# Reordering the block products of the expert loop in a fused scan and routed-expert kernel

## The chip, the cores and the metric

The kernel runs on one core of a Trainium2 chip. A core has a matrix engine (TensorE, PE in the profile, with its weight loads as PEld), a vector engine (VectorE, DVE), a scalar engine (ScalarE, ACT), GpSimd (POOL) and SyncE (SP), which only issues transfers. Each engine executes its own list of instructions in order, and the lists meet at semaphores. The metric is the device time of one execution in microseconds, as the median of several runs; less is better.

## The reference, cut to what matters

The reference is a chunked state-space scan whose output, 3072 rows of 256 numbers, goes into a router with eight experts. Each row goes to the expert whose embedding has the largest cosine with it, through two matrices with a ReLU between them, and is scaled by its gate.

```python
xn = x / (np.linalg.norm(x, axis=-1, keepdims=True) + 1e-06)
logits = xn @ en.T / tau
expert_idx = np.argmax(logits, axis=1)
...
gate_w = probs[np.arange(N), expert_idx]
for e in range(E):
    mask = expert_idx == e
    ...
    h = np.maximum(x[mask] @ w1[e], 0.0)
    out[mask] = gate_w[mask, None] * (h @ w2[e])
```

Here N is 3072, E is 8, `w1[e]` is 256 by 1024 and `w2[e]` is 1024 by 256, all in fp32.

## The kernel before

The scan takes about the first 68 us and the sorting of rows by expert a few more; the change touches nothing there. Then come nine jobs. Job 0 and job 1 are parts of the first expert's rows and use ordinary products. Jobs 2 to 8 are the other seven experts in falling order of size; their row capacities are 416, 408, 400, 384, 368, 356 and 352. The function `expert(k, n, ...)` writes out the work of job n, and I call this "expert n". The order in which its lines stand is the order on every engine: the code records instructions one after the other, and nothing reorders them.

Each of the two matrix products of an expert is done in the Winograd form of Strassen's method: both operands are cut in 2 by 2 blocks, and seven block products stand for eight. This needs sums of blocks beforehand and additions afterwards:

- The first product (x times `w1`). `first_sum(i)`, i from 0 to 3, makes the sums of weight blocks on VectorE (tile `ws1`; number 2 overwrites a block of the weights). `first_tokens(i)` makes the sums of the turned rows `xT` (tile `t1`, in the trace `ts<-xT`). `first_product(p, i)`, i from 1 to 7, is block product i for pair p of the hidden features; a pair is two blocks of 128 hidden features, so a call is four instructions on TensorE in the trace. Products 1, 6, 7 and 4 of a pair go one after the other into the same PSUM region `a`, each on top of the last; 2 goes into `b`; 5 and 3 go into `e`. After each of 1, 6, 7 ScalarE copies `a` out (`first_keep`, line 974); after 4 it writes the ReLU of `a` (line 976). After 2, 5 and 3 VectorE adds such a copy to `b` or `e` (line 980), and ScalarE makes the ReLU in place (`first_relu`, line 986). The next product into a region can't begin before the copy out of it is done.
- The second product (hidden features times `w2`). `weight_sum(i)` and `token_sum(i, g)` make the sums on VectorE, `product(i)` the block products (eight instructions each), and `keep(i)` takes them out: 1, 6, 7 and 4 by ScalarE (lines 1034 and 1036), 2, 5 and 3 by VectorE (line 1040). Its products go in the order 1, 2, 6, 5, 7, 4, 3, so `keep(3)` is the last VectorE operation of an expert.

Around these stand: `past.out(parts)`, which turns the previous expert's result back by transposes on TensorE (line 1050), scales each part of 128 rows by its gate on ScalarE or, for odd parts, on VectorE, and scatters it by an indirect transfer issued by GpSimd (line 1056); part 0 needs only `keep(2)` and `keep(4)`, part 1 also needs `keep(3)`, since 128 to 255 reaches into the second half of the rows. `squares` and `gate_steps` make the gates: ScalarE squares, GpSimd takes a power (line 848), five small VectorE steps, an exponential on ScalarE (line 866), three more VectorE steps. `begin(n + 1)` gathers rows by GpSimd, `ahead.turn_x` turns the gathered rows of the next expert, `left_blocks` is a generator whose small VectorE steps are spread over the experts, and `rest(n)` has SyncE load weights two experts on. In expert 8 a GpSimd `drain` waits until the scatters issued so far have landed.

PSUM has eight banks. Five of them serve both matrix products through a ring, `k.bank["five"]`; three others, `turned`, serve the transposes.

Of the kernel before, what the change touches and what calls it, by code (L numbers as in the profile page):

```python
# [7 lines left out]
F32 = mybir.dt.float32  # L8
# [15 lines left out]
DM, E, F = NH * D, 8, 1024  # L24
# [801 lines left out]
class Job:  # L826
# [102 lines left out]
    def first_sum(s, i):  # L929
        k = s.k  # L930
        if i == 0:
            s.s1 = k.p.tile([128, 3, F // 2], F32, name="ws1", tag="ws1", bufs=1)
        w = lambda m, j: s.w1[:, j, F // 2 * m : F // 2 * m + F // 2]
        s.sums_of(i, [s.s1[:, q] for q in range(3)], w)

# [6 lines left out]
    def first_product(s, p, i):  # L942
        k, h = s.k, s.w // 2
        if p == 0 and i == 1:
            s.hT = k.p.tile([128, KF, CAP], F32, name="hT", tag="hT")
            s.pairs = [Net(), Net()]
        u = s.pairs[p]
        if i in (1, 2, 5):
            t = k.bank["five"]()
            setattr(u, {1: "a", 2: "b", 5: "e"}[i], t[:].rearrange("p (g c) -> p g c", g=2)[:, :, 0:h])  # L950
        w = lambda j, m: s.w1[:, j, F // 2 * m : F // 2 * m + F // 2]
        x = lambda j, n: s.xT[:, j, h * n : h * n + h]
        lhsT, rhs, out = {
            1: (w(0, 0), x(0, 0), "a"), 2: (w(1, 0), x(1, 0), "b"), 3: (s.s1[:, 2], x(1, 1), "e"),
            4: (w(1, 1), s.t1[:, 3], "a"), 5: (s.s1[:, 0], s.t1[:, 0], "e"), 6: (w(0, 1), s.t1[:, 1], "a"),
            7: (s.s1[:, 1], s.t1[:, 2], "a"),
        }[i]
        out = getattr(u, out)
        for g in range(2):
            f = 128 * (2 * p + g)  # L960
            k.nc.tensor.matmul(  # L961
                out[:, g], lhsT=lhsT[:, f : f + 128], rhs=rhs, start=(g == 0 and i in (1, 2, 5)), stop=True,
                skip_group_check=True,
            )
# [40 lines left out]
    def product(s, i, fs=range(KF // 2)):  # L1005
        k, h, half = s.k, s.w // 2, KF // 2
        if i == 1 and 0 in fs:
            s.y2 = [k.bank["five"](), k.bank["five"]()]
        a = s.y2[0][:, 0:h]
        b, e = s.y2[1][:, 0:h], s.y2[1][:, 256 : 256 + h]  # L1010
        out = (a, b, e, a, e, a, a)[i - 1]
# [27 lines left out]
            out, in0, q = {2: (c[0][0], b, 0), 5: (c[1][1], e, 2), 3: (c[0][1], e, 1)}[i]  # L1039
            nc.vector.tensor_tensor(out=out, in0=in0, in1=s.p[:, q], op=ALU.add)  # L1040

    def out(s, which=None):
        k, nc = s.k, s.k.nc
        for i, p in enumerate(s.parts):
            if which is not None and i not in which:
# [3 lines left out]
            for j in range(KD):  # L1049
                nc.tensor.transpose(t[:p, 128 * j : 128 * j + 128], s.yT[:, j, o : o + p], k.ident[:])  # L1050
            y = k.p.tile([128, DM], F32, name="yo", tag="yo", bufs=4)
            if i % 2:
                nc.vector.tensor_scalar_mul(y[:p], t[:p, 0:DM], s.gate[:p, i : i + 1])
            else:
                nc.scalar.activation(y[:p], t[:p, 0:DM], ACT.Copy, scale=s.gate[:p, i : i + 1])  # L1055
# [8 lines left out]
def ring(banks):  # L1064
    state = [0]

    def take():
        state[0] += 1
        return banks[(state[0] - 1) % len(banks)]

    return take
# [6 lines left out]
def moe(k):  # L1078
# [4 lines left out]
    turned = ring([banks[3], banks[6], banks[7]])  # L1083
    k.bank = {
        "hp": ring([banks[2], banks[0], banks[1]]), "xt": turned, "yp": ring(banks[4:6]), "ot": turned,
        "five": ring([banks[0], banks[1], banks[2], banks[4], banks[5]]),
    }
    last = NC - 1
    j0 = jobs[0]
    j0.turn_x(ring(banks[3:5]))  # L1090
# [46 lines left out]
    j = jobs[1]  # L1137
# [21 lines left out]
def expert(k, n, left, begin, rest):  # L1159
    nc, jobs = k.nc, k.jobs  # L1160
    j, past = jobs[n], jobs[n - 1]
    ahead = jobs.get(n + 1)
    j.first_product(0, 1)
    j.first_keep(0, 1)
    j.first_product(0, 2)
    j.first_keep(0, 2)
    j.first_product(0, 6)
    j.first_keep(0, 6)
    j.first_relu(0, 2)
    j.weight_sum(0)  # L1170
    j.first_product(0, 5)
    j.first_product(0, 7)
    j.first_keep(0, 7)
    j.first_keep(0, 5)
    j.first_product(1, 1)
    j.first_keep(1, 1)
    j.first_relu(0, 5)
    j.first_product(0, 4)
    j.first_keep(0, 4)
    j.first_product(1, 2)  # L1180
    j.first_keep(1, 2)
    j.first_product(0, 3)
    j.first_keep(0, 3)
    j.first_product(1, 6)
    j.first_keep(1, 6)
    j.first_relu(0, 3)
    j.first_relu(1, 2)
    j.weight_sum(1)
    j.token_sum(0, 0)
    j.first_product(1, 5)  # L1190
    j.first_product(1, 7)
    j.first_keep(1, 7)
    j.first_keep(1, 5)
    past.out((0, 1))
    j.first_relu(1, 5)
    past.out(range(2, past.nt))
    if n == E:
        nc.gpsimd.drain()
    j.first_product(1, 3)
    j.first_keep(1, 3)  # L1200
    j.first_relu(1, 3)
    j.first_product(1, 4)
    j.first_keep(1, 4)
    j.token_sum(1, 0)
    j.weight_sum(2)
    j.token_sum(0, 1)
    j.token_sum(1, 1)
    if n == E:
        k.blocks = nc.values_load(k.left[0][0:1, 1, 0:1], min_val=0, max_val=LEFT)
    j.product(1)  # L1210
    j.keep(1)
    j.product(2)
    j.keep(2)
    j.squares()
    j.token_sum(2, 0)
    j.token_sum(2, 1)
    if n + 1 < E:
        begin(n + 1)
    j.product(6)
    j.keep(6)  # L1220
    j.weight_sum(3)
    j.product(5)
    j.token_sum(3, 0)
    j.token_sum(3, 1)
    gates = j.gate_steps()
    next(gates)
    j.product(7)
    j.keep(7)
    j.keep(5)
    if ahead:  # L1230
        ahead.turn_x(act=True)
        for i in range(4):
            ahead.first_sum(i)
    j.product(4)
    j.keep(4)
    next(gates, None)
    next(left, None)
    if ahead:
        for i in range(4):
            ahead.first_tokens(i)  # L1240
    if n == E:
        j.product(3, (0, 1))
        j.out((0,))
# [219 lines left out]
```

## Time and profile before

| | us |
|---|---|
| median of 3 runs | 267.79 (267.2 to 269.1) |
| the profiled execution: its time | 267.06 |
| the profiled execution: span from first to last instruction | 265.2 |
| expert 2 begins (first block product) | 97.18 |
| experts 3, 4, 5, 6, 7, 8 begin | 120.33, 143.39, 165.72, 188.75, 210.17, 231.21 |

All times of the trace count from the start of the span. A row of a timeline has the start, the time from the start of its first instruction to the end of its last, the engine, the line, the operation, what is written and read, and the count; in brackets stands how long the engine was idle before it and what ended that. A matmul's end contains its way through the array, so the next one begins before it: the cost of a matmul in a stream is the distance from start to start. `ts` is a sum of rows or of hidden features, `ws` a sum of weight blocks, `hp` and `yp` are the copies that ScalarE takes out, `hT` the hidden features, `yoT` the result before it is turned back.

### The profile page before, as it was taken

The page shows a single profiled execution, that of the slowest core. Times are in us where ns is not written, and L with a number is a line of the kernel's source. Part 1 is how long each engine was busy: PE and PEld are TensorE (multiplying, and loading weights), DVE is VectorE, ACT ScalarE, POOL GpSimd, SP SyncE. Part 2 cuts the span into 40 slices and gives each one's busy share as a digit, 9 for nine tenths or more (in the row PEclk, how much of TensorE's full clock was granted, in tenths as well). Part 3 has the DMA queues.
Part 4 walks back from the last instruction along what each step waited for, and adds up shares of the span by engine and source line. Part 5 has one row for each costly group of instructions (what it writes and reads, how often), then busy time and mean ns, then how long its engine had stood idle before and what let it go on. Part 6 is the DMA issues. An engine that isn't in the chain of part 4 may idle for free. (4 is left out here: it accounts for less than half of the span.)

```text
span 265.2 us, 6638 instructions
## 1 busy us (share of the span) xinstructions
PE 234.0 (88%) x2504; PEld 212.8 (80%) x2504; DVE 194.5 (73%) x546; ACT 125.8 (47%) x313; POOL 98.8 (37%) x125
## 2 busy tenths in 40 slices
PE   7798997887989999899999999799899999979670
PEld 7686876776779999898898989689789888968560
DVE  7899899987783834687688578768958867867420
ACT  4855775754422326634543573364365247246110
POOL 8355314453036342380283068018207405104213
PEclk9999999999999999999999999999999999999978
DMA  5566765653519965335065134506601201000001
GB/s 181 173 211 196 246 209 144 234 165 129 186 31 340 371 205 199 114 127 177 7 218 164 55 107 160 174 0 224 197 18 60 58 0 55 5 0 27 28 2 55
DMA packets 21121, 34.83 MB, mean 131 GB/s; under 512 B 2618, under 2 KB 14112, under 8 KB 21088
## 3 DMA queue, kind: packets, MB, share of 16 engines
q1 hardware_dynamic: 18272, 27.94, 32.5%
q0 software_dynamic: 2592, 6.39, 7.8%
q8 instruction: 20, 0.33, 0.6%
q14 instruction: 13, 0.11, 0.1%
q10 hardware_dynamic: 224, 0.06, 0.1%
HBM read 28.02 MB, written 6.42 MB: 130 GB/s over the span
## 5 line engine op out<-in xcount | busy, mean ns | idle before, releaser
L1056 POOL DMA_INDIRECT out_dram<-yo,to x26 | 27.9, 1071 | 91.2 <-ACT yo L1055 85.6
L980 DVE TENSOR_TENSOR hT<-bank,hp 128x416 f32<-128x416 f32 (+6 forms) x42 | 23.4, 556 | 23.6 <-ACT hp L974 12.3
L974 ACT COPY hp<-bank 128x416 f32<-128x416 f32 (+6 forms) x42 | 20.1, 478 | 40.5 <-PE bank L961 40.3
L833 POOL DMA_INDIRECT xg<-rows,table x24 | 27.0, 1123 | 6.9 <-issue 5.5
L961 PE MATMUL bank<-ts,w 128*128 128x208 f32 (+6 forms) x112 | 24.0, 337 | 6.1 <-DVE ts L927 6.1
L578 POOL TENSOR_SCALAR_AFFINE_SELECT g<-g 128x1024 f32<-128x1024 f32 x17 | 19.4, 1152 | 26.6 <-ACT g L577 26.6
L923 DVE TENSOR_TENSOR ws<-w 128x512 f32<-128x512 f32 x42 | 28.2, 684 | 0.2
L1021 PE MATMUL bank<-ts,w 128*128 128x208 f32 (+6 forms) x112 | 22.3, 345 | 4.1 <-ACT yp L1034 4.1
L961 PEld LDWEIGHTS bank<-ts,w 128*128 128x128 f32 x112 | 18.2, 189 | 9.3 <-issue 6.4
L986 ACT ACTIVATE hT<-hT 128x416 f32<-128x416 f32 (+6 forms) x42 | 21.2, 522 | 6.9 <-DVE hT L980 6.9
L961 PE MATMUL bank<-ts,ws 128*128 128x208 f32 (+6 forms) x112 | 23.1, 339 | 0.0
L1021 PEld LDWEIGHTS bank<-ts,w 128*128 128x128 f32 x112 | 19.2, 199 | 4.7 <-ACT yp L1034 4.3
L961 PE MATMUL bank<-xT,w 128*128 128x208 f32 (+6 forms) x112 | 21.6, 326 | 0.0
L961 PEld LDWEIGHTS bank<-ts,ws 128*128 128x128 f32 x112 | 18.2, 189 | 3.0 <-ACT hp L974 3.0
L1021 PE MATMUL bank<-ts,ws 128*128 128x208 f32 (+6 forms) x112 | 19.3, 326 | 0.0
L1021 PE MATMUL bank<-hT,w 128*128 128x208 f32 (+6 forms) x112 | 19.3, 326 | 0.0
L961 PEld LDWEIGHTS bank<-xT,w 128*128 128x128 f32 x112 | 18.8, 190 | 0.0
L1021 PEld LDWEIGHTS bank<-hT,w 128*128 128x128 f32 x112 | 18.4, 190 | 0.0
L1021 PEld LDWEIGHTS bank<-ts,ws 128*128 128x128 f32 x112 | 18.4, 190 | 0.0
L927 DVE TENSOR_TENSOR ts<-hT 128x416 f32<-128x416 f32 (+6 forms) x28 | 14.9, 554 | 3.0 <-ACT hT L986 3.0
L848 POOL TENSOR_TENSOR gr<-gr,half 128x3 f32<-128x3 f32 (+2 forms) x9 | 10.5, 1169 | 15.3 <-ACT sq L844 10.2
L1040 DVE TENSOR_TENSOR yoT<-bank,yp 128x208 f32<-128x208 f32 (+6 forms) x21 | 7.5, 356 | 11.8 <-PE bank L1021 8.1
(254 smaller groups left out, 516.7 us busy)
## 6 DMA issues: line engine op xcount, KB each, us to landing
w<-in_moe_w_dram SPq DMA_DIRECT2D x14, 1024.0 KB, 5.6
rows<-yt SPq DMA_DIRECT2D x12, 264.0 KB, 2.8
in_x<-in_x_dram SPq DMA_DIRECT2D x6, 512.0 KB, 4.5
w<-in_moe_w_dram SPq DMA_DIRECT2D x8, 256.0 KB, 3.2
in_c<-in_CT_dram SPq DMA_DIRECT2D x6, 256.0 KB, 3.7
in_t<-in_B_dram SPq DMA_DIRECT2D x6, 256.0 KB, 4.9
bz<-in_BT_dram SPq DMA_DIRECT2D x40, 32.0 KB, 3.1
out_dram<-yo,to POOLq DMA_INDIRECT x26, 2.6
```

The lines of the kernel that those rows point to most:

```text
L578: nc.gpsimd.affine_select(out=g, in_=g, pattern=[[0, 8], [1, Q]], compare_op=ALU.is_ge, fill=0.0, base=0, channel_multiplier=-1)
L833: s.k.nc.gpsimd.indirect_dma_start(out=s.x[0:p, i, 0:TOK], out_offset=None, in_=rows, in_offset=bass.IndirectOffsetOnAxis(ap=s.at[0:p, i : ...
L848: nc.gpsimd.tensor_tensor(out=s.r[:], in0=s.r[:], in1=k.half[:, 0:nt], op=ALU.pow)
L923: s.k.nc.vector.tensor_tensor(out=o, in0=in0, in1=in1, op=op)
L927: s.k.nc.vector.tensor_tensor(out=t[i], in0=in0, in1=in1, op=ALU.subtract)
L961: k.nc.tensor.matmul(out[:, g], lhsT=lhsT[:, f : f + 128], rhs=rhs, start=(g == 0 and i in (1, 2, 5)), stop=True, skip_group_check=True,)
L974: nc.scalar.copy(out=u.p[:, {1: 0, 6: 1, 7: 2}[i]], in_=u.a)
L980: nc.vector.tensor_tensor(out=out, in0=in0, in1=u.p[:, q], op=ALU.add)
L986: s.k.nc.scalar.activation(c, c, ACT.Relu)
L1021: k.nc.tensor.matmul(out, lhsT=lhsT, rhs=rhs, start=(i in (1, 2, 5) and f == 0), stop=(f == half - 1), skip_group_check=True)
L1040: nc.vector.tensor_tensor(out=out, in0=in0, in1=s.p[:, q], op=ALU.add)
L1056: d = nc.gpsimd.indirect_dma_start(out=k.out[:, :], out_offset=bass.IndirectOffsetOnAxis(ap=s.to[0:p, i : i + 1], axis=0), in_=y[:p], in_o ...
```

## The change

Every arithmetic operation stays, and so does the number of instructions on TensorE. What is different, in the order of the code:

- The tile of the weight sums `ws1` gets two buffers, so that an expert's sums can be made while the last expert's are still read.
- The five banks are no longer taken from a ring. `k.five` is a list, and each use has its own place in it: `a` of the pairs in places 0 and 3, `b` in 1 and 4, `e` in 2 and 1 (pair 1's `e` takes the bank that pair 0's `b` had). The second product takes places 0 and 4, and then the list is permuted for the next expert.
- The products of both pairs are interleaved in another order: (0,1), (0,2), turned outputs, (0,6), (1,1), (0,5), (0,7), (1,2), (1,6), (0,4), (1,5), (1,7), (0,3), turned outputs, (1,3), (1,4).
- Of the previous expert's outputs, parts 0 and 1 are turned ahead of the sixth product, and the others later; in expert 8 all are turned early, and the drain of GpSimd follows at once. All are scaled on ScalarE.
- Of the next expert's four weight sums, 0 and 1 are made in the first half of the expert before, 2 behind `keep(5)`, 3 behind the next expert's row sums, which move ahead of product 4.
- The squares stand ahead of the second product's product 2. In expert 8 the gates' small steps come behind product 4 instead of ahead of product 7.

The lists of instructions show this at three places. On TensorE, expert 8 from its first product on: line 961 was a first block product, and is line 962 after the change; 1050 turned an output, now 1052; `bank_1432`, `1433`, `1434`, `1436` and `1437` are the five banks. Before:

```order
L961 MATMUL bank_1436<-xT,w_1_67 128x176 x2
L961 MATMUL bank_1437<-xT,w_1_67 128x176 x2
L961 MATMUL bank_1436<-ts,w_1_67 128x176 x2
L961 MATMUL bank_1432<-ts,ws_2898 128x176 x2
L961 MATMUL bank_1436<-ts,ws_2898 128x176 x2
L961 MATMUL bank_1433<-xT,w_1_67 128x176 x2
L961 MATMUL bank_1436<-ts,w_1_67 128x176 x2
L961 MATMUL bank_1434<-xT,w_1_67 128x176 x2
L961 MATMUL bank_1432<-xT,ws_2898 128x176 x2
L961 MATMUL bank_1433<-ts,w_1_67 128x176 x2
L961 MATMUL bank_1436<-ts,ws_2898 128x176 x2
L961 MATMUL bank_1433<-ts,ws_2898 128x176 x2
```

The same place after the change:

```order
L962 MATMUL bank_1433<-xT,w_1_67 128x176 x2
L962 MATMUL bank_1436<-xT,w_1_67 128x176 x2
L1052 MATMUL bank_1439<-ident,yoT 128x128 x2
L1052 MATMUL bank_1435<-ident,yoT 128x128 x2
L1052 MATMUL bank_1438<-ident,yoT 100x128 x2
L962 MATMUL bank_1433<-ts,w_1_67 128x176 x2
L962 MATMUL bank_1432<-xT,w_1_67 128x176 x2
L962 MATMUL bank_1434<-ts,ws_2792 128x176 x2
L962 MATMUL bank_1433<-ts,ws_2792 128x176 x2
L962 MATMUL bank_1437<-xT,w_1_67 128x176 x2
L962 MATMUL bank_1432<-ts,w_1_67 128x176 x2
L962 MATMUL bank_1433<-ts,w_1_67 128x176 x2
```

The outputs of expert 7 moved from behind the twelfth product to behind the second, and two other products, or one and the transposes, now stand between any two products of the same region, where before it was one at most places.

On VectorE, from the end of expert 6 to the first row of expert 7 (923 is a sum of weight blocks, 927 a sum of rows, 869 to 871 the gates' end, 1263 and 1299 a step of `left_blocks`, 1040 the last `keep(3)`). Before:

```order
L923 TENSOR_TENSOR w_0_65<-ws_2730,w_0_65 128x512
L923 TENSOR_TENSOR ws_2730<-w_0_65 128x512
L869 TENSOR_REDUCE gate<-gl 128x3
L870 TENSOR_SCALAR gate<-gate 128x3
L871 RECIPROCAL gate<-gate 128x3
L1263 TENSOR_TENSOR mine_not<-mine,over 128x256
L1299 TENSOR_REDUCE left_n<-mine_not 128x32
L927 TENSOR_TENSOR ts<-xT 128x178
L927 TENSOR_TENSOR ts<-xT,ts 128x178
L927 TENSOR_TENSOR ts<-xT 128x178
L927 TENSOR_TENSOR ts<-xT,ts 128x178
L1040 TENSOR_TENSOR yoT<-bank_1437,yp 128x184
```

Two more sums of weights stood ahead of these rows, behind `keep(5)`. After the change these two are gone from here, and `keep(5)` is followed by:

```order
L923 TENSOR_TENSOR w_0_65<-ws_2615,w_0_65 128x512
L927 TENSOR_TENSOR ts<-xT 128x178
L927 TENSOR_TENSOR ts<-xT,ts 128x178
L927 TENSOR_TENSOR ts<-xT 128x178
L927 TENSOR_TENSOR ts<-xT,ts 128x178
L923 TENSOR_TENSOR ws_2615<-w_0_65 128x512
L869 TENSOR_REDUCE gate<-gl 128x3
L870 TENSOR_SCALAR gate<-gate 128x3
L871 RECIPROCAL gate<-gate 128x3
L1276 TENSOR_TENSOR mine_not<-mine,over 128x256
L1312 TENSOR_REDUCE left_n<-mine_not 128x32
L1042 TENSOR_TENSOR yoT<-bank_1437,yp 128x184
```

The row sums moved ahead of the fourth weight sum, the gates and the left-over step; `keep(3)` is still the last.

On ScalarE, the second product of expert 8 (1034 and 1036 are the copies out of products 1, 6, 7 and 4, 844 the squares, 866 the gates' exponential, 1055 the scaled outputs). Before:

```order
L1034 COPY yp<-bank_1437 128x176
L844 ACTIVATE sq,gr<-xg_329 128x256 x3
L1034 COPY yp<-bank_1437 128x176
L866 ACTIVATE gl<-gl 128x24
L1034 COPY yp<-bank_1437 128x176
L1036 COPY yoT<-bank_1437 128x176
L1055 ACTIVATE yo<-bank_1439,gate 128x256
L1055 ACTIVATE yo<-bank_1438,gate 96x256
```

After the change:

```order
L1036 COPY yp<-bank_1433 128x176
L844 ACTIVATE sq,gr<-xg_329 128x256 x3
L1036 COPY yp<-bank_1433 128x176 x2
L1038 COPY yoT<-bank_1433 128x176
L866 ACTIVATE gl<-gl 128x24
L1057 ACTIVATE yo<-bank_1439,gate 128x256
L1057 ACTIVATE yo<-bank_1438,gate 96x256
```

The exponential moved from ahead of product 7's copy to behind product 4's.

The diff, cut to its core:

```diff
-            s.s1 = k.p.tile([128, 3, F // 2], F32, name="ws1", tag="ws1", bufs=1)
+            s.s1 = k.p.tile([128, 3, F // 2], F32, name="ws1", tag="ws1")
...
         if i in (1, 2, 5):
-            t = k.bank["five"]()
-            setattr(u, {1: "a", 2: "b", 5: "e"}[i], t[:].rearrange("p (g c) -> p g c", g=2)[:, :, 0:h])
+            n, q = {1: ("a", (0, 3)), 2: ("b", (1, 4)), 5: ("e", (2, 1))}[i]
+            t = k.five[q[p]]
+            setattr(u, n, t[:].rearrange("p (g c) -> p g c", g=2)[:, :, 0:h])
...
-            s.y2 = [k.bank["five"](), k.bank["five"]()]
+            s.y2 = [k.five[0], k.five[4]]
+            k.five = [k.five[q] for q in (1, 2, 3, 0, 4)]
...
-            if i % 2:
+            if i % 2 and not act:
                 nc.vector.tensor_scalar_mul(y[:p], t[:p, 0:DM], s.gate[:p, i : i + 1])
...
+    k.five = [banks[i] for i in (2, 0, 1, 4, 5)]
...
+    def ahead_sum(*which):
+        for i in which:
+            if ahead:
+                ahead.first_sum(i)
+
+    product(0, 1)
+    keep(0, 1)
+    product(0, 2)
+    keep(0, 2)
+    early = range(past.nt) if n == E else (0, 1)
+    past.out(early, act=True)
     if n == E:
         nc.gpsimd.drain()
+    j.weight_sum(0)
+    product(0, 6)
+    keep(0, 6)
+    relu(0, 2)
+    j.weight_sum(1)
+    product(1, 1)
+    keep(1, 1)
+    product(0, 5)
+    ahead_sum(0)
+    product(0, 7)
+    keep(0, 7)
+    keep(0, 5)
+    product(1, 2)
+    keep(1, 2)
+    relu(0, 5)
+    product(1, 6)
+    keep(1, 6)
+    relu(1, 2)
+    j.weight_sum(2)
+    product(0, 4)
+    keep(0, 4)
+    ahead_sum(1)
+    product(1, 5)
+    product(1, 7)
+    keep(1, 7)
+    keep(1, 5)
+    product(0, 3)
+    keep(0, 3)
+    relu(1, 5)
+    relu(0, 3)
+    past.out([i for i in range(past.nt) if i not in early], act=True)
+    j.token_sum(0, 0)
+    product(1, 3)
+    keep(1, 3)
+    relu(1, 3)
+    product(1, 4)
+    keep(1, 4)
     j.token_sum(1, 0)
-    j.weight_sum(2)
...
     j.keep(1)
+    j.squares()
     j.product(2)
     j.keep(2)
-    j.squares()
...
     gates = j.gate_steps()
-    next(gates)
+    if n < E:
+        next(gates)
     j.product(7)
     j.keep(7)
     j.keep(5)
+    ahead_sum(2)
     if ahead:
         ahead.turn_x(act=True)
         for i in range(4):
-            ahead.first_sum(i)
+            ahead.first_tokens(i)
     j.product(4)
     j.keep(4)
-    next(gates, None)
+    ahead_sum(3)
+    for _ in gates:
+        pass
     next(left, None)
-    if ahead:
-        for i in range(4):
-            ahead.first_tokens(i)
```

More of the change, by code (lines that the diff above doesn't have):

```diff
@@ L1040, in keep, with out @@
             nc.vector.tensor_tensor(out=out, in0=in0, in1=s.p[:, q], op=ALU.add)
-    def out(s, which=None):
+    def out(s, which=None, act=False):
         k, nc = s.k, s.k.nc
@@ L1085, in moe @@
         "hp": ring([banks[2], banks[0], banks[1]]), "xt": turned, "yp": ring(banks[4:6]), "ot": turned,
-        "five": ring([banks[0], banks[1], banks[2], banks[4], banks[5]]),
     }
+    k.five = [banks[i] for i in (2, 0, 1, 4, 5)]
     last = NC - 1
@@ L1162, in expert @@
     ahead = jobs.get(n + 1)
[L1163 to L1196, printed above, removed]
+    product, keep, relu = j.first_product, j.first_keep, j.first_relu
+    def ahead_sum(*which):
[8 more added lines that the diff above has]
+    past.out(early, act=True)
     if n == E:
         nc.gpsimd.drain()
[L1199 to L1203, printed above, removed]
+    j.weight_sum(0)
[35 more added lines that the diff above has]
+    keep(1, 4)
     j.token_sum(1, 0)
-    j.weight_sum(2)
     j.token_sum(0, 1)
@@ L1220, in expert @@
     j.keep(6)
+    j.token_sum(3, 0)
+    j.token_sum(3, 1)
     j.weight_sum(3)
     j.product(5)
-    j.token_sum(3, 0)
-    j.token_sum(3, 1)
     gates = j.gate_steps()
-    next(gates)
+    if n < E:
+        next(gates)
     j.product(7)
```

## The prediction

> **What bounds the kernel now.** I read the page's busy shares first, then who waited for whom from 97 us on, where the changed code begins.
>
> ```profile
> PE 234.0 (88%) x2504; PEld 212.8 (80%) x2504; DVE 194.5 (73%) x546; ACT 125.8 (47%) x313; POOL 98.8 (37%) x125
> PEclk9999999999999999999999999999999999999978
> ```
>
> ```profile
> PE bank L961 <- DVE ts L927: 6.1, 6, 1.8
> PE bank L1021 <- ACT yp L1034: 4.1, 1, 4.1
> PE bank L961 <- DVE hT L980: 2.2, 4, 0.8
> PE bank L1050 <- ACT yo L1055: 0.9, 3, 0.3
> ```
>
> TensorE is the bound, and the time is the sum of its products and of its waits. The products stay, so the change can only take waits away or bring new ones. There are four kinds: six waits for sums of rows (6.1 us), one of 4.1, and 2.2 + 0.9 = 3.1 us around the outputs and product (1,3). The fourth kind isn't in this list because each is too short; TensorE's timeline shows it. Rows are starts of experts 4 to 7, expert 3 from its sixth product to its outputs, and expert 8 from its start to product (1,3):
>
> ```profile
> 122.08 0.93 PE L961 MATMUL bank<-ts,w 128*128 128x204 f32 x4 [0.21 <-DVE ts L927]
> ...
> 127.32 0.85 PE L961 MATMUL bank<-ts,w 128*128 128x204 f32 x4
> 128.01 1.71 PE L961 MATMUL bank<-ts,ws 128*128 128x204 f32 x8
> 129.55 0.71 PE L1050 MATMUL bank<-ident,yoT 128*128 128x128 f32 x5
> ...
> 143.39 1.52 PE L961 MATMUL bank<-xT,w 128*128 128x200 f32 x8
> ...
> 165.72 1.46 PE L961 MATMUL bank<-xT,w 128*128 128x192 f32 x8
> ...
> 188.75 1.41 PE L961 MATMUL bank<-xT,w 128*128 128x184 f32 x8
> ...
> 210.17 1.37 PE L961 MATMUL bank<-xT,w 128*128 128x178 f32 x8
> ...
> 231.21 1.36 PE L961 MATMUL bank<-xT,w 128*128 128x176 f32 x8
> 234.01 0.83 PE L961 MATMUL bank<-ts,w 128*128 128x176 f32 x4 [1.45 <-DVE ts L927]
> ...
> 236.09 0.76 PE L961 MATMUL bank<-xT,w 128*128 128x176 f32 x4
> 236.79 0.86 PE L961 MATMUL bank<-ts,w 128*128 128x176 f32 x4
> ...
> 238.09 0.76 PE L961 MATMUL bank<-xT,ws 128*128 128x176 f32 x4
> 238.69 0.76 PE L961 MATMUL bank<-ts,w 128*128 128x176 f32 x4
> 239.28 1.57 PE L961 MATMUL bank<-ts,ws 128*128 128x176 f32 x8
> 240.69 0.82 PE L1050 MATMUL bank<-ident,yoT 128*128 128x128 f32 x6
> 241.95 0.86 PE L961 MATMUL bank<-xT,ws 128*128 128x176 f32 x4 [0.45 <-DVE hT L980]
> ```
>
> A block product that waits for nothing takes 238.69 - 238.09 = 0.60 us in expert 8, and 128.01 - 127.32 = 0.69 in expert 3. But (1,1), at 236.09, is followed only 0.70 later by (0,4), and the pair (1,5), (1,7) takes 1.41 instead of 1.19: a product into a region waits for ScalarE's copy of the one before, and one product between them doesn't cover it. These gaps are the fourth kind.
>
> **The change, part by part.** *Gaps between products.* From the sixth product to the outputs stand ten products. Expert 8 takes 240.69 - 234.01 = 6.68 us for them, against 10 x 0.595 = 5.95: 0.73 lost. Expert 3 takes 7.47 against 6.9: 0.57. With 0.65 as the mean, seven experts lose 4.5 us. After the change at least two products stand between two of the same region, 1.2 us in expert 8. The wait to be covered is what one product and its gap last, 0.70, plus 0.1 to 0.2 where ScalarE is late. The tightest place is (1,7): the copy of (1,6) now stands on ScalarE behind ReLU (0,5), which waits for VectorE; copy, addition, ReLU and copy of some 0.5 us each from (0,7) on are 2.0, and TensorE has four products, 2.4, to do. So I take the whole 4.5; bounds: 0 (the copies come late all the same) and 4.5.
>
> *The sixth product's wait.* It ends with VectorE's sums of rows, which stand in that engine's queue behind four sums of weights, the gates and a step of the left-over table. Two of the four sums leave, and the row sums go ahead of the rest, so this wait goes: 6.1 us. Late next is `keep(3)`, still the last in the queue, and now the turned outputs stand ahead of the sixth product and wait for it. These are its rows at the ends of experts 3 to 7, and two sums of weights at the end of expert 6:
>
> ```profile
> 145.72 0.36 DVE L1040 TENSOR_TENSOR yoT<-bank,yp 128x204 f32<-128x204 f32 x1
> ...
> 169.28 0.36 DVE L1040 TENSOR_TENSOR yoT<-bank,yp 128x200 f32<-128x200 f32 x1
> ...
> 191.46 0.35 DVE L1040 TENSOR_TENSOR yoT<-bank,yp 128x192 f32<-128x192 f32 x1
> ...
> 207.82 1.28 DVE L923 TENSOR_TENSOR ws<-w 128x512 f32<-128x512 f32 x2
> ...
> 212.95 0.34 DVE L1040 TENSOR_TENSOR yoT<-bank,yp 128x184 f32<-128x184 f32 x1
> ...
> 234.29 0.34 DVE L1040 TENSOR_TENSOR yoT<-bank,yp 128x178 f32<-128x178 f32 x1
> ```
>
> Without two sums it comes 1.3 us sooner. At the start of expert 8 it then ends at 234.29 - 1.33 + 0.34 = 233.30; TensorE gets to part 1 at 231.21 + 1.19 for two products + 0.22 for part 0 (0.82 for six transposes, the last one's end included) = 232.62. The wait is 0.68, with the way between engines 0.74. Likewise at experts 5, 6 and 7: 1.13, 0.32 and 0.46; at expert 4 it ends before TensorE comes (144.75 against 144.97), and at expert 3, whose wait was the shortest, I take none. New waits: 2.65 us, so 6.1 - 2.65 = 3.45 are gained. The longest is at expert 5, behind the longest left-over step. Bounds: 6.1 gained if the outputs wait for nothing, 0 if they wait as long as the sixth product did.
>
> *Around product (1,3).* It waits for VectorE's addition (1,5), which needs ScalarE's copy of (1,7). From the end of (1,7)'s issue to (1,3) were 241.95 - 240.69 = 1.26 us in expert 8. In that time TensorE now does (0,3), 0.60, and what outputs are left: none in expert 8 (wait 0.66) and in expert 2 (0.7, its products being longer), one part in experts 6 and 7 (0.44 each), two in 3 to 5 (0.25 each). That is 3.0 us against 3.1: nothing gained. The 0.9 us behind scaled outputs, inside these 3.1, go because four parts no longer stand together on three banks.
>
> *The end of expert 8.* TensorE's product 7, the stop, product 4, and the first half of product 3 with the outputs behind it; GpSimd's last scatter and its power; ScalarE's copy; and the stretch behind the stop with its clock:
>
> ```profile
> 246.83 2.55 PE L1021 MATMUL bank<-ts,ws 128*128 128x176 f32 x16
> 253.44 2.65 PE L1021 MATMUL bank<-ts,w 128*128 128x176 f32 x8 [4.05 <-ACT yp L1034]
> 255.88 1.29 PE L1021 MATMUL bank<-hT,ws 128*128 128x176 f32 x4
> 257.01 0.38 PE L1050 MATMUL bank<-ident,yoT 128*128 128x128 f32 x2
> ```
>
> ```profile
> 244.98 1.34 POOL L1056 DMA_INDIRECT out_dram<-yo,to  x1 [0.30 <-ACT yp L1034]
> 251.42 0.88 POOL L848 TENSOR_TENSOR gr<-gr,half 128x3 f32<-128x3 f32 x1 [5.11 <-issue]
> ```
>
> ```profile
> 253.10 0.29 ACT L1034 COPY yp<-bank 128x176 f32<-128x176 f32 x1
> ```
>
> ```profile
> 253.40:257.00 3.60, 3.56 (x12) 3.56 (x13) 0.77 (x4) 0.31 (x1) 0.00 (x0) 0.53 0.02 5
> ```
>
> The drain holds GpSimd for 5.11 us; behind it stands the power, behind that the gates, behind these on ScalarE the exponential, and behind that the copy of product 7 for which product 4 waits. Moved ahead of the sixth product, the outputs begin at 232.4 of the old count instead of 240.69, so scatters and drain come some 8 us sooner, and the exponential no longer stands ahead of the copy. What is left is the copy itself: no transposes stand between products 7 and 4 here, so product 4 waits for the end of product 7, the copy of 0.29 and the way to and fro, about 0.55. Gained: 4.05 - 0.55 = 3.5. And product 4 with half of product 3 took 257.01 - 253.44 = 3.57 us, at a granted clock of 0.53; at full clock it is 12 instructions of 0.149 = 1.79, as in the rest of the expert. Without the stop the clock should stay, which gains 1.78 more. By the Trainium skill (TensorE: Matmul & The Clock Gate, the clock gate, what is actually happening) an idle window of about 3.4 us halves the clock, so a wait of 0.55 would leave it whole; the trace agrees with its 4.05 us idle and its 0.53. By this rule the 1.78 belong to the sum; if the clock fell for another reason, the sum would be 1.78 less. Against it, the gates' end now comes behind product 4, and the first output needs it; I take 0.3 off, half of the 0.60 that half a product 3 lasts (bounds 0 and 0.6). Together 3.5 + 1.78 - 0.3 = 5.0.
>
> *Edits at nothing.* Two sums of weights, 1.3 us, enter the first half of each expert, where VectorE waits for ScalarE and TensorE anyway (the additions of line 980 come one per 1.2 us of products). The weights must have landed by then:
>
> ```profile
> L191 SPq DMA_DIRECT2D w<-in_moe_w_dram x7: 378/378/396, 78.6 to 179.0; - x7
> DMA to landing us min/median/max: 5.2/5.4/8.1
> ```
>
> The last is issued at 179.0, lands by 187.1, and its sums now begin at the start of expert 7, after 210: over 20 us to spare. Outputs that VectorE scaled go to ScalarE, which is busy 47% of the span. The second buffer of `ws1` and the earlier squares cost nothing: the squares stand on ScalarE beside product 2, as beside product 6 before.
>
> *Sum.* 4.5 + 3.45 + 0 + 5.0 = 12.95 us. The profiled execution's time is 267.06, so 254.1; the median of the runs shown lies 0.7 above it, and I forecast 254.5 for the median after.
>
> **The rivals.** *The wait only moves.* `keep(3)` might be no earlier than the row sums were, since two sums more delay what stands behind them in the first half. The sixth product's 6.1 us would come back at the outputs: 254.5 + 3.45 = 258.0. Against it: the rows above.
>
> *The gaps stay,* because ScalarE's queue gets the scaled outputs ahead of the sixth product's copy and ReLUs that wait for VectorE ahead of others: 254.5 + 4.5 = 259.0. For it: ScalarE has 18 operations of about 0.45 us in the 9 us of the first half.
>
> *The drain still holds the power.* If GpSimd comes late all the same, the first output waits for the gates by what is left of the 4 us; the clock stays down too: 254.5 + 5.0 = 259.5. Against it: the scatters start some 8 us sooner and the drain lasts 5.11.
>
> *Slower.* The outputs hold TensorE and, through the scaled output ahead of the sixth product's copy, ScalarE. If the row sums find `xT` not yet copied out (the copies stand on ScalarE behind the exponential and the copy of product 7), VectorE stops with the fourth sum, the gates and `keep(3)` behind it, and both other engines stop with it. It decides from 2.6 us more at each of six starts, where the time is 254.5 + 16 = 270. The Trainium skill (TensorE: Matmul & The Clock Gate, queue depths) calls ScalarE's and VectorE's queues strictly first in, first out; the copy at 253.10 behind an idle ScalarE agrees. Against the rival: the exponential depends on nothing that is later than before.
>
> **How the numbers follow.** Chances: forecast 0.66, the wait only moves 0.10, the gaps stay 0.09, the drain 0.05, slower 0.03, and 0.07 that the outputs wait for nothing, 6.1 instead of 3.45, with some more at the joins, 251.5. The range takes in all but the drain and the slower case, and of the gaps case the better half: 251.0 to 258.9. A measurement of this kernel tells about 1% from no change. Faster by over 1%: 0.93; within 1%: 0.04; slower: 0.03.
>
> **What would show it.** In the profile after, products (0,6) to (1,7) spaced at 0.60 to 0.70; no wait for sums of rows, but waits of the first outputs for `yoT` of about 2.7 us in all, the longest at expert 5; waits before (1,3) of 3 us; no idle over 1 us before product 4 of expert 8, and a full clock behind it. A starved sixth product, a clock of 0.5 at the end, or waits at the outputs over 1.2 us would make me wrong.

## The result, and the profile after

The changed kernel takes 257.36 us (median of 4 runs, 254.6 to 258.23); the kernel before, run beside it on the same chip, 268.45 us (267.2 to 269.69). The ratio is 0.957, with an interval of 0.948 to 0.966. The forecast was 254.5, with a range of 251.0 to 258.9. The profiled execution took 258.23 us, with a span of 256.4. Here and below, ratios leave out executions over 1.5% above the fastest of their kernel; medians and ranges take in all.

These are, from the page, busy shares and the row of TensorE's clock in 40 slices, and then the list of TensorE's waits from 97 to 262 us (engine, tile and line, what it waited for: us in total, times, longest):

```profile
PE 233.6 (91%) x2504; PEld 215.9 (84%) x2504; DVE 188.7 (74%) x536; ACT 129.0 (50%) x323; POOL 97.5 (38%) x125
...
PEclk9999999999999999979999999999999999999997
```

```profile
PE bank L962 <- ACT hp L975: 2.0, 1, 2.0
PE bank L1052 <- DVE yoT L1042: 1.7, 3, 0.8
PE bank L962 <- DVE hT L981: 1.2, 4, 0.5
PE bank L1023 <- ACT yp L1036: 0.4, 1, 0.4
```

Nobody waits for sums of rows any more, and of 4.1 us before product 4 of expert 8, 0.4 is left. The waits for `yoT` are new and short. But there is a wait of 2.0 us for `hp` that no part of the forecast had, and a 7 in the clock's row where the expert loop should run at full clock.

TensorE's timeline shows the same places as before: the starts of experts 2 to 8, expert 5 with its outputs, and expert 8 up to product (0,3) and at its end:

```profile
100.05 1.57 PE L962 MATMUL bank<-xT,w 128*128 128x208 f32 x8
...
126.28 1.54 PE L962 MATMUL bank<-xT,w 128*128 128x204 f32 x8
...
170.30 0.38 PE L1052 MATMUL bank<-ident,yoT 128*128 128x128 f32 x2
171.52 0.44 PE L1052 MATMUL bank<-ident,yoT 128*128 128x128 f32 x2 [0.84 <-DVE yoT L1042]
...
229.10 1.36 PE L962 MATMUL bank<-xT,w 128*128 128x176 f32 x8
230.30 0.38 PE L1052 MATMUL bank<-ident,yoT 128*128 128x128 f32 x2
231.12 0.66 PE L1052 MATMUL bank<-ident,yoT 128*128 128x128 f32 x4 [0.44 <-DVE yoT L1042]
231.61 0.76 PE L962 MATMUL bank<-ts,w 128*128 128x176 f32 x4
232.21 0.76 PE L962 MATMUL bank<-xT,w 128*128 128x176 f32 x4
232.81 1.36 PE L962 MATMUL bank<-ts,ws 128*128 128x176 f32 x8
234.00 0.76 PE L962 MATMUL bank<-xT,w 128*128 128x176 f32 x4
234.59 1.36 PE L962 MATMUL bank<-ts,w 128*128 128x176 f32 x8
235.79 1.36 PE L962 MATMUL bank<-ts,ws 128*128 128x176 f32 x8
236.98 0.76 PE L962 MATMUL bank<-xT,ws 128*128 128x176 f32 x4
```

```profile
246.07 1.46 PE L1023 MATMUL bank<-ts,w 128*128 128x176 f32 x8 [0.39 <-ACT yp L1036]
247.37 0.76 PE L1023 MATMUL bank<-hT,ws 128*128 128x176 f32 x4
247.96 0.38 PE L1052 MATMUL bank<-ident,yoT 128*128 128x128 f32 x2
...
249.38 0.66 PE L1052 MATMUL bank<-ident,yoT 128*128 128x128 f32 x4 [0.43 <-DVE yoT L1042]
```

TensorE's last row in the kernel before:

```profile
258.42 0.66 PE L1050 MATMUL bank<-ident,yoT 128*128 128x128 f32 x4 [0.43 <-DVE yoT L1040]
```

From 231.61 to 236.98 are nine products in 5.37 us, 0.597 each: the gaps are gone. Product 4 and half of product 3 take 247.96 - 246.07 = 1.89 us where they took 3.57.

The two spans differ by 265.2 - 256.4 = 8.8 us, and they can be split by the starts of the experts. Expert 3 to the end of TensorE's work took 138.75 us before (120.33 to 259.08) and takes 123.76 now (126.28 to 250.04): 15.0 gained. Three stretches gave back 6.2. From TensorE's end to the end of the span it is 6.4 us instead of 6.15. Expert 2 lasts 26.23 us instead of 23.15, 3.1 more, where 0.65 less was forecast. And expert 2 starts at 100.05 instead of 97.18, 2.9 later, behind a scan whose code is the same. The experiments had to say what of these 6 us belongs to the change.

### The profile page after: what moved, and what is told of

It reads as the page before. It is cut to its first block, busy times and chain, and to the rows that moved or that the text cites. A ratio compares the mean times of both kernels' runs of the same rounds, so it can differ in the third digit from the quotient of the medians.

```text
span 256.4 us, 6619 instructions
## 1 busy us (share of the span) xinstructions
PE 233.6 (91%) x2504; PEld 215.9 (84%) x2504; DVE 188.7 (74%) x536; ACT 129.0 (50%) x323; POOL 97.5 (38%) x125
## 5 line engine op out<-in xcount | busy, mean ns | idle before, releaser
L981 DVE TENSOR_TENSOR hT<-bank,hp 128x416 f32<-128x416 f32 (+6 forms) x42 | 22.1, 552 | 22.4 <-ACT hp L975 17.7
L578 POOL TENSOR_SCALAR_AFFINE_SELECT g<-g 128x1024 f32<-128x1024 f32 x17 | 18.8, 1119 | 28.6 <-ACT g L577 28.6
L987 ACT ACTIVATE hT<-hT 128x416 f32<-128x416 f32 (+6 forms) x42 | 21.6, 524 | 13.5 <-DVE hT L981 13.5
L962 PE MATMUL bank<-ts,w 128*128 128x208 f32 (+6 forms) x112 | 21.9, 327 | 2.0 <-ACT hp L975 2.0
L962 PE MATMUL bank<-ts,ws 128*128 128x208 f32 (+6 forms) x112 | 22.0, 341 | 0.1
L848 POOL TENSOR_TENSOR gr<-gr,half 128x3 f32<-128x3 f32 (+2 forms) x9 | 9.8, 1085 | 31.0 <-ACT sq L844 31.0
L1023 PE MATMUL bank<-ts,w 128*128 128x208 f32 (+6 forms) x112 | 21.1, 331 | 0.4 <-ACT yp L1036 0.4
L962 PEld LDWEIGHTS bank<-ts,w 128*128 128x128 f32 x112 | 18.3, 190 | 2.4 <-ACT hp L975 2.3
L962 PEld LDWEIGHTS bank<-ts,ws 128*128 128x128 f32 x112 | 19.5, 198 | 0.5 <-ACT hp L975 0.5
L1023 PE MATMUL bank<-ts,ws 128*128 128x208 f32 (+6 forms) x112 | 19.3, 326 | 0.0
L1023 PEld LDWEIGHTS bank<-ts,w 128*128 128x128 f32 x112 | 18.2, 190 | 1.0 <-ACT yp L1036 0.7
L1023 PEld LDWEIGHTS bank<-ts,ws 128*128 128x128 f32 x112 | 18.4, 190 | 0.0
L561 PE MATMUL pgA<-cp,bz 32*128 32x128 f32 x192 | 14.6, 293 | 2.3 <-DVE cp L296 1.9
```

What stands on the lines that cost most here:

```text
L561: k.nc.tensor.matmul((k.pgA, k.pgB)[q // 2][:, q % 2, a : a + 128], lhsT=t.bz[r, v, b + i, :], rhs=t.cp[r, b + i, :], start=True, stop=Tru ...
L578: nc.gpsimd.affine_select(out=g, in_=g, pattern=[[0, 8], [1, Q]], compare_op=ALU.is_ge, fill=0.0, base=0, channel_multiplier=-1)
L848: nc.gpsimd.tensor_tensor(out=s.r[:], in0=s.r[:], in1=k.half[:, 0:nt], op=ALU.pow)
L962: k.nc.tensor.matmul(out[:, g], lhsT=lhsT[:, f : f + 128], rhs=rhs, start=(g == 0 and i in (1, 2, 5)), stop=True, skip_group_check=True,)
L981: nc.vector.tensor_tensor(out=out, in0=in0, in1=u.p[:, q], op=ALU.add)
L987: s.k.nc.scalar.activation(c, c, ACT.Relu)
```

## The experiments

The time from the start of expert 2 to TensorE's end, which the expectations use, leaves the scan out. It was 161.9 us before, 150.0 in the profile above, and 147.4 in the first repeat of the changed kernel.

### The changed kernel again

To tell chance from change I ran the changed kernel twice more, unaltered, beside the other experiments.

> The changed kernel unaltered, to see whether its run repeats. In the profile after, expert 2 lost 1.96 us before product (0,4) and then ran 3.4 us at half clock, and the scan ended 2 us later than before. If both are chance (theory), the loss in expert 2 is not there in this profile, the granted clock has no dip before the last 10 us, and the span is 252 to 253 us. If the loss belongs to the new order (rival), the 1.9 to 2.0 us stand at the same product again and the span is 255 to 257 us.

> The changed kernel unaltered, on the same chip as the three others, so that expert 2 can be compared. All theories: 255 to 258, expert 2 at 23.7 us, or at 25 to 26.4 in a profile with the stop of about 2 us in it.

The first gave 256.33 us (ratio 0.952, 0.945 to 0.960), the second 254.56 (0.940, 0.933 to 0.946). From expert 3 to TensorE's end the profiles took 123.70 and 123.76 us, so the 15.0 us are there each time. Expert 2 lasted 23.68 and 23.67 us, and the wait of 2.0 us was absent: of the 3.1 us, 0.5 comes back every time, and 2.5 come with a stop that these two profiles don't have. It is not a matter of the first profile alone: of the eight profiles of this study with early outputs in expert 2, four have it.

Expert 2 started at 99.33 and 99.13. Over all profiles it starts anywhere from 97.2 to 102.4, and most of this goes with the clock in the scan. In the first profile after, the granted clock became full at 10.6 us, in the kernel before at 4.4; the matmuls of line 218 stand 0.21 us apart between 4.5 and 10 us in the one and 0.11 in the other, long before any changed line. In two other profiles it also became full late (10.5 us in `a_out2_again`, 13.5 in `a_gates`), and these three start expert 2 at 99.5 to 102.4. In four it fell to half once between 42 and 70 us (both repeats, `a_keep3_first`, `a_out2_late`; start 98.4 to 100.1). Of the seven with neither, the three with the outputs at the old place start at 97.2 to 98.3, the four with other orders at 97.9 to 99.3. So I count the later start as chance.

### The new order of products alone

The kernel before, with the new interleaving and the banks by name; the next expert's sums, squares, gates and drain as they were, and the outputs still behind the twelfth product. (The sums for the second product that stand inside the interleaving moved with it.)

```diff
-    j.first_product(0, 6)
-    j.first_keep(0, 6)
-    j.first_relu(0, 2)
     j.weight_sum(0)
-    j.first_product(0, 5)
-    j.first_product(0, 7)
...
+    product(0, 6)
+    keep(0, 6)
+    relu(0, 2)
+    j.weight_sum(1)
+    product(1, 1)
+    keep(1, 1)
+    product(0, 5)
+    product(0, 7)
...
```

> The kernel before with the new interleaving of the block products and the banks named by use, and nothing else: outputs, sums, squares, gates and drain stay where they were. Theory (the gaps between products are worth 4.5 us): products (0,6) to (0,3) stand 0.60 apart in expert 8, from the start of expert 2 to the last instruction of TensorE it takes 161.9 - 4.5 = 157.4 us, the ratio to the kernel before is 0.983. Waits of the sixth product stay at about 6.1 us and the one before product 4 of expert 8 at 4.1. Rival (the copies come late all the same, the gaps stay): 161.9 us, ratio 1.00. Third case (with the gaps gone TensorE comes sooner to other waits): between 158 and 161, with longer waits for hT, yo or the sums of rows; then part of the gaps' gain depends on the other parts of the change.

It took 263.43 us, ratio 0.979 (0.972 to 0.986); from the start of expert 2 to TensorE's end 157.5 us, 4.4 gained where 4.5 were expected. Its waits, those before the sixth products and before product 4 of expert 8, then the sixth product of expert 5 in TensorE's timeline, then two stretches there, with the granted clock last but two in a row, behind the busy times:

```profile
PE bank L962 <- DVE ts L927: 6.4, 6, 2.1
PE bank L1023 <- ACT yp L1036: 4.1, 1, 4.1
```

```profile
163.76 1.46 PE L962 MATMUL bank<-xT,w 128*128 128x192 f32 x8
167.36 0.89 PE L962 MATMUL bank<-ts,w 128*128 128x192 f32 x4 [2.14 <-DVE ts L927]
```

```profile
165.30:167.30 2.00, 0.00 (x0) 0.00 (x0) 1.51 (x5) 0.00 (x0) 0.00 (x0) 1.00 1.02 353
169.01:172.37 3.36, 3.36 (x14) 3.36 (x14) 0.74 (x3) 1.14 (x3) 0.00 (x0) 0.58 0.00 0
```

The waits for sums of rows and the stop stay, as they should. The sum agreed partly by luck. Added up from the starts of single matmuls, the gaps of the kernel before were 0.45 us in expert 2 and 0.63 in expert 8, 3.8 over seven experts, not 4.5; here none over 0.1 us is left outside expert 2 and the slow stretch. The waits before (1,3) shrank too, by some 3.4 us over the seven experts. Against that, the wait of 2.14 us in expert 5 was followed by 3.4 us at a clock of 0.58, which made that expert 1.15 us longer than before. At the end of expert 8 the clock stayed low for 6.8 us instead of 3.4, which cost some 0.7 more.

### The sums of weights at their old place

The changed kernel, with sums 0 and 1 behind `keep(5)` again.

```diff
     product(0, 5)
-    ahead_sum(0)
...
-    ahead_sum(1)
     product(1, 5)
...
     j.keep(5)
-    ahead_sum(2)
+    ahead_sum(0, 1, 2)
```

> The changed kernel with the next expert's sums of weights 0 and 1 put back behind the addition of product 5, with number 2. Theory (VectorE's queue up to the addition of product 3 sets the wait of the first outputs): that addition comes 1.3 us later, the waits of the first outputs grow from 1.7 us in all to 8 or 9, and the time rises by 6 to 7 us over the changed kernel. Rival (these sums were hidden at either place): it rises by less than 1.5 us.

```profile
PE bank L1052 <- DVE yoT L1042: 8.8, 7, 2.2
```

The outputs wait 8.8 us instead of 1.7, and from the start of expert 2 to TensorE's end it is 154.66 us, 7.3 more than in the first repeat. (Its runs spread from 260.13 to 268.02 us, too wide for a ratio.) So the two sums carry this part of the gain. Without them, the row sums' earlier place would only have moved the wait to the outputs, which is the forecast's first rival.

### `keep(3)` first

The changed kernel, with `keep(3)` ahead of the gates' end, the fourth sum and the left-over step in experts 2 to 7.

```diff
-    ahead_sum(3)
-    for _ in gates:
-        pass
-    next(left, None)
...
     j.keep(3)
+    if n < E:
+        for _ in gates:
+            pass
+        ahead_sum(3)
+        next(left, None)
```

> The changed kernel with the addition of product 3 put ahead of the gates' end, the fourth sum of weights and the left-over step on VectorE, in experts 2 to 7. Theory: the first outputs wait for nothing but the addition itself, and their 1.7 us go; the time falls by 1.5 us or a little less. Rival: what was ahead now delays the addition of product (0,2) by 1 to 2 us, ScalarE stops before its ReLU with the copies behind it, and as much is lost within the first half: 0 or up to 3 us slower than the changed kernel.

It took 255.13 us (ratio 0.950, 0.940 to 0.960), and 145.27 from the start of expert 2 to TensorE's end, 2.1 less than the first repeat, where at most 1.5 was expected: that was the sum of listed waits, which leaves part of their cost out (see below). At the start of expert 8, all six transposes now follow one another:

```profile
225.06 1.36 PE L962 MATMUL bank<-xT,w 128*128 128x176 f32 x8
226.25 0.82 PE L1052 MATMUL bank<-ident,yoT 128*128 128x128 f32 x6
```

The waits for `yoT` at the starts of experts 5 and 8 are gone. (In time alone, 2.1 us are within the intervals of the two kernels.) This confirms what stood in front of `keep(3)` as their cause.

### The drain alone

The kernel before, with only the turned outputs and the drain of expert 8 moved ahead of the sixth product. The outputs' scatters, for which the drain waits, move with it, so the run tests both together.

```diff
     j.first_keep(0, 2)
+    if n == E:
+        past.out()
+        nc.gpsimd.drain()
     j.first_product(0, 6)
...
```

> The kernel before, with one part of the change alone: in expert 8 the outputs of expert 7 and the drain stand behind product (0,2). The gates keep their old place. Theory (the drain held the power, the power the gates, these the copy of product 7): the 4.05 us before product 4 of expert 8 fall under 0.7, the clock behind it stays full, and the time falls by 5 us, to 0.981 of before. Rival (the gates would come late all the same, from the squares): the wait stays over 2 us and the time falls by less than 2.

It took 264.75 us, ratio 0.984 (0.976 to 0.992). Product 4 of expert 8, the clock behind it, and the new wait:

```profile
252.09 1.46 PE L1021 MATMUL bank<-ts,w 128*128 128x176 f32 x8 [0.52 <-ACT yp L1034]
```

```profile
252.00:255.60 3.60, 3.07 (x20) 2.80 (x21) 1.11 (x5) 0.82 (x3) 0.43 (x1) 1.00 0.02 5
```

```profile
PE bank L1050 <- DVE yoT L1040: 2.3, 2, 1.9
```

The stop and the slow clock go with this edit alone; expert 8 up to TensorE's end is 4.1 us shorter. It is not more, because without the moved sums the outputs wait 1.9 us for `keep(3)`, where the sixth product had waited 1.45, and product (1,3) waits 1.1 instead of 0.45.

### The gates back ahead of product 7

```diff
-    if n < E:
-        next(gates)
+    next(gates)
```

> The changed kernel with expert 8's five gate steps and the exponential ahead of product 7 again, as before the change; the outputs and the drain stay early. Theory (the stop before product 4 came from the drain, and the gates' new place only delays the first output): product 4 waits for no more than 0.4 us, the clock behind it stays full, and the first scaled output of the last expert starts 0.3 to 0.4 us sooner behind its transposes. Rival (the exponential in ScalarE's queue ahead of product 7's copy made the stop): product 4 waits 1 us or more.

One run took 259.26 us, with expert 2 starting at 102.36 and the 2.0 us wait in it; so I read its end alone:

```profile
247.40 1.46 PE L1023 MATMUL bank<-ts,w 128*128 128x176 f32 x8 [0.52 <-ACT yp L1036]
248.69 0.76 PE L1023 MATMUL bank<-hT,ws 128*128 128x176 f32 x4
...
249.71 0.47 ACT L1057 ACTIVATE yo<-bank,gate 128x256 f32<-128x256 f32 x1 [0.51 <-PE bank L1052]
```

Product 4 waits 0.52 us, so the exponential ahead of the copy was not what made the stop. The first output is scaled 249.71 - 248.69 = 1.02 us behind the start of product 3; in the first repeat it is 245.38 - 244.04 = 1.34. The gates' new place therefore costs the first output 0.32 us, and saves TensorE 0.12.

### Product (1,4) ahead of (1,3)

```diff
-    product(1, 3)
-    keep(1, 3)
-    relu(1, 3)
-    product(1, 4)
-    keep(1, 4)
     j.token_sum(1, 0)
+    product(1, 4)
+    keep(1, 4)
+    product(1, 3)
+    keep(1, 3)
+    relu(1, 3)
```

> The changed kernel with block product (1,4) ahead of (1,3), so that a product stands between the addition (1,5) and (1,3). Theory (the waits before (1,3) can be covered): the 1.2 us of waits for hT in experts 4 to 8 go; from the start of expert 2 to the end of TensorE 147.4 - 1.2 = 146.2, ratio to the kernel before 0.948 where the changed kernel had 0.952. Rival (the ReLU of (1,3) now stands last, and the sums of hidden features behind it are late for product 6): the waits go from (1,3) to product 6, 147.4 or more.

It took 257.26 us (ratio 0.959, 0.952 to 0.965). The waits for `hT` are gone from its list, and yet experts 3 to 8 are only 0.1 to 0.2 us shorter than in the three profiles of the changed kernel. (Expert 2 had the stop of 2 us here, so the time from its start can't be compared with what was expected.) Products 1 and 2, 6, and 5 and 7 of expert 7, here and then in the changed kernel:

```profile
218.40 2.58 PE L1023 MATMUL bank<-hT,w 128*128 128x178 f32 x16
220.98 1.80 PE L1023 MATMUL bank<-ts,w 128*128 128x178 f32 x8
222.62 2.58 PE L1023 MATMUL bank<-ts,ws 128*128 128x178 f32 x16
```

```profile
219.88 2.58 PE L1023 MATMUL bank<-hT,w 128*128 128x178 f32 x16
222.29 1.37 PE L1023 MATMUL bank<-ts,w 128*128 128x178 f32 x8
223.50 2.58 PE L1023 MATMUL bank<-ts,ws 128*128 128x178 f32 x16
```

From product 1 to product 5 it is 4.22 us against 3.62: product 6, twice, waits for sums of hidden features that now come later. The rival held, the wait had only moved.

### Expert 2's outputs later

```diff
-    early = range(past.nt) if n == E else (0, 1)
+    early = range(past.nt) if n == E else (0, 1) if n > 2 else ()
```

> The changed kernel with all of expert 2's turned outputs at the later place, as in the experts' first half before. Theory (the early outputs, which run beside the four gathers of GpSimd there, make ScalarE's copies late): expert 2 lasts 23.65 - 0.9 = 22.8 us, and the copies that came 0.9 to 1.4 us behind the modelled end of their matmuls come at once. Rival (the new interleaving itself does it, or the loading of weights at that time): it stays at 23.6.

> The changed kernel with expert 2's outputs at the later place, a second time and now timed. Theory (the early outputs cost expert 2 between 1.5 us and 4 us, by chance): a time of 253 to 254.5, 2 to 4 us below the changed kernel in the same comparison, and a narrower spread of its runs; expert 2 lasts 22.2 us again. Rival (the first profile of it was a lucky run): as the changed kernel, about 257, with expert 2 at 23.6 or more.

The single run took 252.49 us; four more took 253.54 (252.4 to 253.82; ratio 0.940, 0.935 to 0.946). Expert 2 lasted 22.21 us (98.37 to 120.58) and 22.25 (99.53 to 121.78), 1.4 less than in the repeats of the changed kernel and 0.9 less than before, where the gaps promised 0.65. So the early outputs, and not the new order, make expert 2 late; `b_order`, with the outputs at the old place, has 22.21 too. In time, where 2 to 4 us were expected, this can't be told from the unaltered kernel of the same comparison, whose ratio is 0.940 as well.

### Only its scatters later

In expert 2 the outputs are turned and scaled early, and the lines that scatter them stand behind product (0,3).

```diff
-    past.out(early, act=True)
+    later = []
+    past.out(early, act=True, later=later if n == 2 else None)
...
+    for part in later:
+        past.scatter(*part)
```

> The changed kernel where, in expert 2 alone, the outputs are turned and scaled at the early place, and only their two scatters are issued at the later place, behind product (0,3). Theory (the scatters, issued by GpSimd right behind the four gathers, hold up the others): expert 2 lasts 22.2 us, as with the outputs late. Rival (the transposes and ScalarE's two scalings ahead of the sixth product's copy do it): 23.6 us or more. Between them (22.6 to 23.2): the long stop of some profiles is the scatters', the first us is not.

Expert 2 lasted 25.93 us, with the stop, and the time was 254.38 us. But the edit did not do what it says. The scatters of the old place begin beyond 107 us; here GpSimd began the first as soon as its gathers were done:

```profile
102.87 1.03 POOL L1065 DMA_INDIRECT out_dram<-yo,to  x1 [0.30 <-ACT hT L987]
...
106.26 0.51 ACT L975 COPY hp<-bank 128x416 f32<-128x416 f32 x1 [3.03 <-PE bank L962]
...
106.82 0.97 PE L962 MATMUL bank<-ts,w 128*128 128x208 f32 x4 [2.00 <-ACT hp L975]
```

Nothing else stands between gathers and scatters in GpSimd's own list, so the later line left them where they were. The run doesn't tell scatters from transposes.

### The two gains together

Both edits, `keep(3)` first and expert 2's outputs later.

> The changed kernel with the two edits that gained: keep(3) ahead of the fourth weight sum, the gates' end and the left-over step in experts 2 to 7 (measured -2.1 us from the start of expert 2 to the end of TensorE), and expert 2's outputs at the later place (-1.5 to -4). Theory (the two are independent): 147.4 - 2.1 - 1.5 = 143.8 us from the start of expert 2 to the end of TensorE, a time of 251 to 252, ratio to the kernel before 0.935. Rival (with keep(3) sooner the later outputs of expert 2 wait at another place): 145 or more, a time above 253.

```profile
PE bank L962 <- DVE hT L981: 1.1, 3, 0.5
PE bank L1052 <- DVE yoT L1042: 0.4, 1, 0.4
PE bank L1023 <- ACT yp L1036: 0.4, 1, 0.4
```

It took 250.40 us (249.91 to 252.2, 6 runs), ratio 0.932 (0.927 to 0.937), against 254.56 for the changed kernel in the same comparison, whose interval just overlaps (0.933 to 0.946); 143.85 us from the start of expert 2 to TensorE's end, as the sum of the two had it. Its three kinds of waits amount to 1.9 us.

## Why the prediction was right

From expert 3 on the mechanisms were the named ones, and the median lies 2.9 us above the forecast, inside the range. That it lies so near is in part luck, since two deviations in opposite directions nearly cancel: experts 3 to 8 gained more than forecast, expert 2 and the scan took some back. (The forecast's own sum, 254.1 and 0.7 for the median, makes 254.8 and not 254.5.) This table compares, from expert 3 on, TensorE's time between starts over the time of an undisturbed product or transpose:

| place | before | after | gained | forecast |
|---|---|---|---|---|
| between products, (0,6) to (0,3) | 3.3 | 0.0 | 3.3 | 3.9 |
| sixth product, or first outputs | 7.5 | 2.3 | 5.2 | 3.45 |
| before (1,3), less the transposes | 3.9 | 2.9 | 1.0 | 0 |
| product 4 of expert 8, wait and clock | 6.0 | 0.7 | 5.3 | 5.3 |
| sum | | | 14.8 | 12.6 |

**The gaps** were 3.8 us over seven experts and not 4.5; they went wholly, by `b_order` and by the nine products above. Part of what I had counted as gap belongs to the restart behind the sixth product's wait.

**The sixth product's wait** is where the sum was mis-sized. The step that failed is "6.1 - 2.65 = 3.45 are gained": the 6.1 came from the list of waits, the 2.65 from distances of starts. The list counts a wait from the modelled end of the last matmul. In expert 5 before, two products of 0.65 us each from 165.72 on end their issue at 167.02, and the sixth started at 168.98: 1.96 us lost, where the list has 1.8.

```profile
168.98 0.89 PE L961 MATMUL bank<-ts,w 128*128 128x192 f32 x4 [1.79 <-DVE ts L927]
```

With the restart behind it, six waits of 6.1 us cost 7.5. The new waits came out as forecast by their own measure, 2.3 us instead of 2.65 over the four experts named, the longest at expert 5. `a_sums_late` and `a_keep3_first` show that the two sums and the queue ahead of `keep(3)` set them.

**Around (1,3)** the same mixture of measures hid 1.0 us: 3.1 before was listed idle, 3.0 after was worked out from starts. From expert 3 on it is 3.9 before and 2.9 after.

**The end of expert 8** came as forecast: 0.39 us of wait instead of 0.55, and the clock whole. The 1.78 us for the clock, which went into the sum by the row at 0.53, came out at 3.57 - 1.89 = 1.68, and the gates' delay was 0.32 for a forecast of 0.3. `b_drain_early` and `a_gates` put the stop down to the drain, with the scatters that it waits for, and not to the exponential.

**Expert 2** was the missing mechanism. I gave it a gain of 0.65 us from its gaps and no new wait; it lost 0.5 in each repeat and 3.1 in the first profile. By the runs with late outputs, the early place costs it 1.4 us, and 2.9 to 4.1 where the stop comes, in four of eight profiles. Whether the scatters or the turning and scaling of the outputs do it, no run tells.

**The chances.** The gaps, the drain and the moved wait were the rivals with a price. The first two fell by runs of their own; the moved wait held for 2.3 of 7.5 us, as the forecast had it, and `a_sums_late` shows what it would have been without the two sums. That the time would be slower had no sign in any run.

## What to carry to other kernels

Take what a wait costs on the bounding engine from the distance of starts, before and after alike; a list of idle times is shorter by the way through the array and by the restart, here about a quarter of a microsecond each time. When work is moved to the same place of a loop's every turn, look at each turn's neighbours: what is free in turns 3 to 8 stood in turn 2 beside four gathers. And if an addition behind a queue of unrelated small operations is what the next product waits for, put it first: `keep(3)` first was worth 2.1 us of TensorE's time, by one profile against another, with no other change.

## What the runs showed of the hardware

**A stop that ends with a scatter.** In expert 2 of the first profile after, all four engines stand still until ScalarE goes on with a copy for which TensorE's product, by its modelled end, was ready 103.30 + 1.98 = 105.28, 2.8 us before (products (0,5) and (0,7), GpSimd's first scatter, the copy, and the next product that waits for it):

```profile
103.30 1.98 PE L962 MATMUL bank<-ts,ws 128*128 128x208 f32 x8
...
104.71 1.03 POOL L1058 DMA_INDIRECT out_dram<-yo,to  x1 [0.30 <-ACT hT L987]
...
108.11 0.51 ACT L975 COPY hp<-bank 128x416 f32<-128x416 f32 x1 [2.42 <-PE bank L962]
...
108.67 0.97 PE L962 MATMUL bank<-ts,w 128*128 128x208 f32 x4 [1.96 <-ACT hp L975]
```

The copy starts 108.11 - 104.71 = 3.40 us behind the scatter, and in `a_scatter2_late` 106.26 - 102.87 = 3.39. In all eight profiles with early outputs in expert 2, ScalarE or VectorE ended a wait for TensorE 3.38 to 3.40 us behind the start of that scatter, also where the wait was short. In experts 3 to 8, where the gathers are done before the scatter, there is no such stop. That the scatter's landing releases what TensorE had finished is a reading of this coincidence; no run moved the scatter away from the gathers with the outputs early, and why it is so stays open.

**The clock can fall after a stop of 2 us.** In the first profile after, the stop of 1.96 us is followed by 3.4 us at half clock:

```profile
109.60:113.00 3.40, 3.40 (x12) 3.26 (x11) 1.40 (x4) 1.98 (x5) 0.00 (x0) 0.50 0.00 0
```

So it was after 2.14 us of idle time in `b_order`, 2.00 in `a_scatter2_late` and 1.94 in `a_swap34`; after 2.24 in `a_sums_late`, 2.00 in `a_gates`, 1.90 in `b_drain_early` and 1.79 in the kernel before, it stayed whole. The Trainium skill (TensorE: Matmul & The Clock Gate, the clock gate, what is actually happening) tells of about 3.4 us of idle time as the window that throttles, and of a window that runs freely. The length of the slow stretch agrees; the idle time that sets it off can be shorter here.

Where a stop falls explains most of it. In the traces' clock records, the times between two changes of the clock are whole multiples of 3.413 us: in the first profile after, 29 of them at full clock ahead of the slow stretch, one in it, 41 behind it. On this grid the four stops that were followed by half clock lie each within one step, and the clock falls at the end of that step. Those in `a_sums_late`, the longest of all, in `b_drain_early` and in the kernel before lie across two steps. The stop in `a_gates` doesn't fit: all but 0.04 us of it lies within one step, and the clock stayed whole, so how much idle time in a step it takes stays open. This adds to the spread of the changed kernel's times, 252.8 to 258.2 over three comparisons.
